# Attention and mixer kernel: the score products of tile i + 2 in front of the value products of tile i

## Chip, cores and metric

The kernel runs on one core of a Trainium2 chip. The metric is the device time of one execution in microseconds (us). Lower is better.

## What is computed

The inputs are q, k and v of 8 batches, 8 heads, 576 positions and 64 channels, and four weight matrices. All are float32, and so is the result.

```python
scores = scale * np.matmul(q, k.transpose(0, 1, 3, 2))
mask = (rel >= 0) & (rel < 64)             # rel = query position - key position
attn = softmax(np.where(mask, scores, -1e9))
x = np.matmul(attn, v)                     # heads side by side: (8, 576, 512)
xt = x.transpose(0, 2, 1)
u = x + (np.maximum(xt @ w_tok1, 0.0) @ w_tok2).transpose(0, 2, 1)
out = u + np.maximum(u @ w_ch1, 0.0) @ w_ch2
```

Each query sees the 64 positions up to its own, so a block of 64 queries needs two blocks of 64 keys.

## The kernel before

**Tiles.** The first stage (the first 256 us) is the attention with the token mixer. It goes over 36 tiles of 128 query rows, numbered 0 to 35. A tile holds two blocks of 64 queries, for all 8 heads. Every ninth tile, with `i % 9 == 4` (4, 13, 22, 31), is shared by two batches: one block of each. The rest of the kernel is the channel mixer, made of large matrix products.

**Steps of one tile**, with the lines that the rows below carry:

- `qk(i)` (L282): the scores, 16 products on quarters of the array (64 rows by 64 columns), into the two PSUM tiles `s`. There are two such buffers of each kind, tag "s".
- `softmax` (L297): VectorE masks the scores and takes the maximum; `softmax_exp` (L305): ScalarE takes the exponentials `e` and their sums.
- `pt_transpose` (L312, L314): TensorE transposes `e` into `pp`, ScalarE copies `pp` to SBUF as `pt`.
- `av(i)` (L324): 16 value products `xp <- v, pt` on halves of the array (128 rows by 64 columns), into the one PSUM buffer `xp`.
- `norm` (L341): VectorE multiplies `xp` with the reciprocals (L335, L336) of the sums, giving `x`.
- `split_x`: ScalarE casts `x` to its high half `xhi` (L109), GpSimd subtracts for the low half `xlo` (L112). In the shared tiles ScalarE makes two casts of 64 rows (L352), one into `xhi` and one into `xlo`, and GpSimd fills the other halves (L353).
- `tok1` (L372): TensorE multiplies `xhi` and `xlo` with the first token weights into the PSUM tiles `h`. When a batch is done, ScalarE and VectorE split `h` (L383, L392).
- a piece of `tok2` (L413, L420): two or three transposes of `x` and six products go into one PSUM buffer `up`; ScalarE copies it out (L425). There is one `up` buffer in this stage, so the first transpose of a piece waits for ScalarE's copy of the piece before it.

Beside this, VectorE, GpSimd and ScalarE convert weights from 64-bit floats and split them (lines L204 to L221, `w1hi`, `w1lo`).

**Order.** Each engine runs its instructions in the order of the program text; nothing reorders them. One round `i` of the loop over tiles issues, on TensorE: transposes of tile i, one piece (A), `tok1` of tile i - 1, value products of tile i, scores of tile i + 2, a second piece (B). On VectorE a round has the softmax of tile i + 1, reciprocals, weight conversion, `norm(i)`, and, where a batch is done, the low half of `h`. On ScalarE it has the two copies to `pt`, a cast of weights, four exponentials of tile i + 1, the copy of piece A, four more exponentials, the cast(s) of `x` of tile i, the copy of piece B. `TOK2_FROM` is 9: the round from which `tok2` pieces run by default.

The two calls that matter stand like this, with the line of `qk` behind that of `av`:

```python
if 0 <= i < NT:
    norm(i, av(i, pts), ri)
finish_h_low()
...
if i + 2 < NT:
    qk(i + 2)
```

Of the kernel before, what the change touches and what calls it, by code (L numbers as in the profile page):

```python
# [27 lines left out]
NT = NPAIR * TPP  # L28
# [17 lines left out]
TOK1_FROM, TOK1_SLOW, TOK2_FROM = 2, 7, 9  # L46
# [34 lines left out]
def tile_blocks(i):  # L81

    p, t = divmod(i, TPP)
    if t == 4:
        return (2 * p, 8), (2 * p + 1, 8)
    b, t = (2 * p, t) if t < 4 else (2 * p + 1, t - 5)
    return (b, t), (b, t + 4)
# [3 lines left out]
def mixer_kernel(ctx: ExitStack, tc: tile.TileContext, qh, kh, vh, wt1, wt2, wc1, wc2, out):  # L91
# [39 lines left out]
    with ExitStack() as actx:  # L131
# [8 lines left out]
        def load_k(i):  # L140
            p, t = divmod(i, TPP)
            if t in (0, 4):
                b = 2 * p + (t == 4)
                kbs[b] = pq.tile([P, NBLK + 1, H // 2, BLK], F32, name=f"k{b}", tag="k", bufs=2)
                if b != 0:
                    nc.sync.dma_start(kbs[b], kh[b])

        def load_q(i):
            qr = pq.tile([P, H // 2, 2, BLK], F32, name=f"q{i}", tag="q", bufs=5)
            nc.sync.dma_start(qr, qh[i])  # L150
            loaded[i] = [qr, None]

        def load_v(i):
            vt = pq.tile([P, 2, H, D], F32, name=f"v{i}", tag="v", bufs=3)
            nc.sync.dma_start(vt, vh[i])
            loaded[i][1] = vt
# [54 lines left out]
        def to_f32_b(c, low, high, n, tag, late):  # L211

            r = cpool[0].tile([P, CW], I32, name=f"r{tag}", tag="cvr", bufs=1)[:, :n]
            w = cpool[0].tile([P, CW], F32, name=f"w{tag}", tag="cvw", bufs=2)[:, :n]
            cf, rf = c.bitcast(F32), r.bitcast(F32)
            nc.vector.scalar_tensor_tensor(out=c, in0=high, scalar=-0x40000000, in1=c,
                                           op0=ALU.bitwise_and, op1=ALU.bitwise_or)
            nc.vector.tensor_scalar(out=r, in0=c, scalar1=-0x800000, scalar2=None, op0=ALU.bitwise_and)
            nc.vector.scalar_tensor_tensor(out=rf, in0=low.bitcast(U32), scalar=2.0 ** -52, in1=rf,  # L219
                                           op0=ALU.mult, op1=ALU.mult)  # L220
            (nc.vector if late else nc.gpsimd).tensor_add(w, rf, cf)  # L221
            return w
# [23 lines left out]
        def job_convert_b():  # L246
            if to_convert_b:
                n, part = to_convert_b.pop(0)
                to_finish.append((n, to_f32_b(*part)))
# [19 lines left out]
        def qk(i):  # L269

            qt = loaded[i][0]
            s = []
            for u in range(2):

                s.append(ps.tile([P, 4, P], F32, name=f"s{i}_{u}", tag="h" if i == 1 else "s", bufs=2))
                s_ps[i, u] = s[u]
            for j in range(4):
                for u in range(2):
                    r = slice(u * BLK, (u + 1) * BLK)
                    for half, (b, n) in enumerate(tile_blocks(i)):  # L280
                        so = s[u][half * BLK:(half + 1) * BLK, j].rearrange("p (n c) -> p n c", n=2)
                        nc.tensor.matmul(so, qt[r, j, half], kbs[b][r, n:n + 2, j],  # L282
                                         start=True, stop=True)

        def softmax(i, u):
            if u == 0:
                st[i] = (pa.tile([P, H], F32, name=f"nm{i}", tag="nm", bufs=3),
                         pa.tile([P, H], F32, name=f"sum{i}", tag="sum", bufs=3))
            nm, sm = st[i]
            mk = mask[1 if tile_blocks(i)[0][1] == 0 else 0]  # L290
            e = pa.tile([P, 4, P], F32, name=f"e{i}_{u}", tag="e", bufs=4)
            e_sb[i, u] = e

            s = s_ps.pop((i, u))
            for h in range(4):
                g = 2 * h + u
                nc.vector.tensor_tensor_reduce(out=e[:, h], in0=s[:, h], in1=mk, scale=-scale, scalar=MAX_F32,  # L297
                                               op0=ALU.add, op1=ALU.min, accum_out=nm[:, g:g + 1])
# [9 lines left out]
        def pt_transpose(i, u):  # L308
            pp = ps.tile([P, 4, P], F32, name=f"pp{i}_{u}", tag="pt")
            e = e_sb.pop((i, u))  # L310
            for h in range(4):
                nc.tensor.transpose(pp[:, h], e[:, h], ident)  # L312
            pt = pa.tile([P, 4, P], F32, name=f"pt{i}_{u}", tag="ptsb", bufs=4)
            nc.scalar.copy(pt, pp)  # L314
            return pt
# [117 lines left out]
        def store_u():  # L433
            while stores:
                us, g0, n = stores.pop(0)
                a = 0
                while a < n:
                    j, o = divmod(g0 + a, CHUNK)
                    m = min(n - a, CHUNK - o)
                    (nc.sync if g0 < (B - 1) * S - 320 else nc.scalar).dma_start(u_dram[j][:, :, o:o + m], us[:, :, a:a + m])  # L440
                    a += m
# [16 lines left out]
        def run_pieces(k):  # L458
            for _ in range(min(k, len(pieces))):
                tok2(*pieces.pop(0))  # L460
# [22 lines left out]
        for i in range(-1, NT + 1):  # L483
            if 0 <= i and i + 2 < NT:
                load_v(i + 2)
            if 3 <= i + 3 < NT:
                load_q(i + 3)
            if i + 4 < NT:
                load_k(i + 4)
            store_u()  # L490
            n_jobs = JOBS[i]
            if i == NT - 1:
                up_tags += [("s", 2), ("pt", 2)]
            have = len(pieces)
            n_pieces = PIECES.get(i, (1, 1) if i >= TOK2_FROM else (0, 0))
            pts = []
            if 0 <= i < NT:
                pts.append(pt_transpose(i, 0))
                if i < NT - 1:
                    pts.append(pt_transpose(i, 1))  # L500
            if i + 1 < NT:
                softmax(i + 1, 0)
            if i + 1 < NT:
                softmax(i + 1, 1)
            if 0 <= i < NT:
                ri = recip(i)
            if i >= N_START:
                while to_finish:
                    job_finish()
            for n in tok1_plan.get(i + 1, ()):  # L510
                last_use = n - NX + ((n - NX) % TPP == 4)
                if n < i and last_use not in tok1_plan.get(i, ()):
                    split_x(n)
            while to_finish:
                job_finish()
            if i + 1 < NT:
                softmax_exp(i + 1, 0)
            run_pieces(min(have, n_pieces[0]))
            have = min(have, len(pieces))
            if i >= N_START:  # L520
                for _ in range(n_jobs):
                    job_convert_a()
            if i == NT - 1:
                pts.append(pt_transpose(i, 1))
            if i < N_START:
                softmax_exp(i + 1, 1)
            for n in tok1_plan.get(i, ()):
                tok1(n)
            if N_START <= i < NT - 1:
                softmax_exp(i + 1, 1)  # L530
            if i >= N_START:
                for _ in range(n_jobs):
                    job_convert_b()
            if 0 <= i < NT:
                norm(i, av(i, pts), ri)
            finish_h_low()
            if i < N_START:
                for _ in range(n_jobs):
                    job_convert_a()
                    job_convert_b()  # L540
            if i + 2 < NT:
                qk(i + 2)
            for n in tok1_plan.get(i + 1, ()):
                if n not in xhl:
                    split_x(n)
            run_pieces(min(have, n_pieces[1]))
            while to_load and len(to_convert) < 2 and i < NT - 2:
                job_load()
            if i == NT - 1:
                while to_convert or to_convert_b or to_finish:  # L550
                    job_convert_a()
                    job_convert_b()
                    job_finish()
                qctx.close()
                pu = uctx.enter_context(tc.tile_pool(name="pu", bufs=1, side="right", reuse_waits="tile"))
                ul = {0: load_u(0, pu)}
# [537 lines left out]
```

## Time and profile before

| | |
|---|---|
| median of 3 runs | 806.01 us (804.53 to 806.02) |
| the profiled execution, its own time | 806.01 us |
| its span, first to last instruction | 804.1 us |
| TensorE products (PE) busy | 789.7 us, 98% of the span |
| TensorE weight loads (PEld) busy | 655.2 us, 81% |
| VectorE (DVE) busy | 567.8 us, 71% |
| ScalarE (ACT) busy | 388.4 us, 48% |
| GpSimd (POOL) busy | 265.1 us, 33% |
| mean granted TensorE clock | 0.999 |

All times are counted from the first instruction. The shares are means over the whole kernel; in the first stage ScalarE and VectorE are much fuller than in the rest. A row of the timeline gives the start, the length, the engine and line, what is written and read, a count of merged instructions, and in brackets how long the engine sat idle before it and what ended that. TensorE's products are pipelined: the spacing of two starts says what a product costs, not its length. A product of float32 operands shows as two records.

### The profile page before, as it was taken

The numbers are of one execution on the slowest core, as the hardware profiler recorded it, in microseconds if no ns is written. First come the engines' busy times: TensorE is split into PE (matmuls) and PEld (weight loads), VectorE is DVE, ScalarE is ACT, GpSimd is POOL, SyncE is SP. The second block draws the span as 40 slices with busy tenths as digits, with TensorE's granted clock in tenths as the row PEclk, the third lists the DMA queues.
The fourth block names the chain that finished last, engine by engine and source line by source line (L and its number), as shares of the span: only waits on it lengthen the run. The fifth ranks groups of instructions, "written<-read, shape, count | busy, mean of one in ns | idle before, by whom it ended". The sixth has DMA issues, their size and how long they took to land. (4 is left out here: it accounts for less than half of the span.)

```text
span 804.1 us, 15810 instructions
## 1 busy us (share of the span) xinstructions
PE 789.7 (98%) x5749; PEld 655.2 (81%) x5749; DVE 567.8 (71%) x1529; ACT 388.4 (48%) x1124; POOL 265.1 (33%) x241
## 2 busy tenths in 40 slices
PE   8999999999999999999999999999999999999997
PEld 6667888888889878888878888888888888888886
DVE  5978789589572895777787474756666666656576
ACT  6998889889874440323334141326332244324040
POOL 3634544445330000000000050549832648723140
PEclk9999999999999999999999999999999999999999
DMA  9856778768635637877555775764985755965543
GB/s 352 274 183 227 231 252 302 236 211 297 218 113 169 198 102 213 255 227 236 196 170 179 281 287 183 246 239 170 315 327 206 287 187 166 364 228 190 199 161 104
DMA packets 86828, 180.59 MB, mean 225 GB/s; under 512 B 8800, under 2 KB 51808, under 8 KB 84832
## 3 DMA queue, kind: packets, MB, share of 16 engines
q1 hardware_dynamic: 84640, 177.76, 64.1%
q10 hardware_dynamic: 2112, 1.84, 0.7%
q8 instruction: 45, 0.74, 0.4%
q14 instruction: 31, 0.25, 0.1%
HBM read 137.69 MB, written 41.88 MB: 223 GB/s over the span
## 5 line engine op out<-in xcount | busy, mean ns | idle before, releaser
L913 PE MATMUL gp<-m,w1hi 128*128 128x512 f32 x504 | 155.8, 390 | 0.4 <-POOL m L794 0.4
L112 POOL TENSOR_TENSOR m7lo<-t3g,m7hi 128x512 fp32r<-128x512 f32 x18 | 23.4, 1302 | 359.5 <-ACT m7hi L109 359.5
L305 ACT ACTIVATE e<-e,nm 128x128 f32<-128x128 f32 x288 | 112.3, 399 | 6.1 <-DVE nm L297 6.1
L913 PEld LDWEIGHTS gp<-m,w1hi 128*128 128x128 f32 x504 | 94.7, 188 | 20.9 <-POOL m L794 1.3
L913 PE MATMUL gp<-m,w1lo 128*128 128x512 f32 x252 | 98.2, 389 | 0.0
L958 DVE TENSOR_TENSOR uf<-op,uf 128x512 f32<-128x512 f32 (+1 forms) x91 | 61.9, 684 | 40.5 <-PE op L969 30.7
L297 DVE CUSTOM_DVE_ANT_0 e<-s,mask 128x128 f32<-128x128 f32 x288 | 63.5, 286 | 12.2 <-PE s L282 12.1
L305 ACT ACTIVATION_READ_ACCUMULATOR e<-e,nm 128x1 f32 x288 | 56.5, 196 | 0.0
L112 POOL TENSOR_TENSOR xlo<-x,xhi 128x512 fp32r<-128x512 f32 x32 | 41.2, 1287 | 46.0 <-ACT xhi L109 45.7
L635 PE MATMUL gp<-uhi,w1hi 128*128 128x512 f32 x144 | 56.1, 389 | 0.0
L635 PE MATMUL gp<-ulo,w1hi 128*128 128x512 f32 x144 | 56.1, 389 | 0.0
L635 PE MATMUL gp<-uhi,w1lo 128*128 128x512 f32 x144 | 56.1, 389 | 0.0
L913 PEld LDWEIGHTS gp<-m,w1lo 128*128 128x128 f32 x252 | 47.3, 188 | 9.7
L643 PE MATMUL op<-ghi,w2hi 128*128 128x512 f32 x128 | 50.0, 390 | 0.9 <-ACT ghi L622 0.9
L643 PE MATMUL op<-glo,w2hi 128*128 128x512 f32 x128 | 50.0, 390 | 0.2 <-DVE glo L623 0.2
L643 PE MATMUL op<-ghi,w2lo 128*128 128x512 f32 x128 | 49.9, 389 | 0.0
L916 ACT COPY x<-gp 128x512 f32<-128x512 f32 x18 | 10.6, 587 | 81.2 <-PE gp L913 81.2
L221 POOL TENSOR_TENSOR w<-r,c 128x384 f32<-128x384 f32 (+1 forms) x28 | 27.6, 985 | 60.5 <-DVE r L219 58.5
L324 PEld LDWEIGHTS xp<-v,pt 128*64 128x64 f32 x1152 | 36.6, 138 | 12.9 <-ACT e L305 10.1
L341 DVE TENSOR_TENSOR x<-xp,ri 128x512 f32<-128x512 f32 x36 | 24.8, 690 | 30.3 <-PE xp L324 29.7
L312 PE MATMUL pp<-ident,e 128*128 128x128 f32 x288 | 44.6, 281 | 1.4
L420 PE MATMUL up<-t2hi,hhi 128*128 128x320 f32 (+1 forms) x128 | 43.0, 336 | 0.0
(204 smaller groups left out, 2042.4 us busy)
## 6 DMA issues: line engine op xcount, KB each, us to landing
v<-vh SPq DMA_DIRECT2D x36, 512.0 KB, 3.8
w1hi<-w1s SPq DMA_DIRECT2D x18, 896.0 KB, 4.9
w1lo<-w1s SPq DMA_DIRECT2D x18, 896.0 KB, 6.9
w1hi<-w2s SPq DMA_DIRECT2D x18, 896.0 KB, 4.6
w1lo<-w2s SPq DMA_DIRECT2D x18, 896.0 KB, 6.4
raw<-wc SPq DMA_DIRECT2D x32, 384.0 KB, 4.4
q<-qh SPq DMA_DIRECT2D x36, 256.0 KB, 4.9
k<-kh SPq DMA_DIRECT2D x7, 1280.0 KB, 8.3
```

The costliest lines, as they stand in the source:

```text
L112: eng_lo.tensor_sub(lo, src, hi.bitcast(F32))
L221: (nc.vector if late else nc.gpsimd).tensor_add(w, rf, cf)
L297: nc.vector.tensor_tensor_reduce(out=e[:, h], in0=s[:, h], in1=mk, scale=-scale, scalar=MAX_F32, op0=ALU.add, op1=ALU.min, accum_out=nm[:, ...
L305: nc.scalar.activation(e[:, h], e[:, h], AF.Exp, bias=nm[:, g:g + 1], scale=-1.0, accum_out=sm[:, g:g + 1])
L312: nc.tensor.transpose(pp[:, h], e[:, h], ident)
L324: nc.tensor.matmul(xp[half * BLK:(half + 1) * BLK, h], pts[h % 2][:, h // 2, half * BLK:(half + 1) * BLK], vt[:, half, h], start=True, sto ...
L341: nc.vector.tensor_mul(x, xp, ri.unsqueeze(2).to_broadcast([P, H, D]))
L420: nc.tensor.matmul(up[:, :n], hx[:, cs], w[:, tt * S + s0:tt * S + s0 + n], start=False, stop=(k == 6), skip_group_check=True)
L635: nc.tensor.matmul(gp, w[:, w1_at(ft, ct)], x[:, ct], start=(k == 0), stop=(k == 3 * NCT - 1))
L643: nc.tensor.matmul(op, w[:, ct, ft], x[:, cols], start=(first and k == 0), stop=(last and k == 3 * len(gs) - 1), skip_group_check=not (fir ...
L913: nc.tensor.matmul(b[INTO[m]], w[:, at], c[:, h, t], start=(k < 4 and z == y == 0), stop=(z == 1 and y == 2), skip_group_check=True)
L958: eng.tensor_add(x, y, x)
```

## The change

From round 9 on, the scores of tile i + 2 are issued before the value products of tile i, and not behind them. In rounds before the ninth nothing changes.

```diff
             if i >= N_START:
                 for _ in range(n_jobs):
                     job_convert_b()
+            if i >= TOK2_FROM and i + 2 < NT:
+                qk(i + 2)
             if 0 <= i < NT:
                 norm(i, av(i, pts), ri)
             finish_h_low()
...
-            if i + 2 < NT:
+            if i < TOK2_FROM and i + 2 < NT:
                 qk(i + 2)
```

On TensorE, in round 22, these rows stand before the change between the last `tok1` product and piece B (a name's first number is the tile, `s24_0` is a score tile of tile 24, `xp22` the value products of tile 22):

```order
L324 MATMUL xp22_2791<-v22_2485,pt22_0_2733 64x64 x8
L324 MATMUL xp22_2791<-v22_2485,pt22_1_2740 64x64 x8
L282 MATMUL s24_0_2810<-k5_2229,q24_2612 64x128 x2
L282 MATMUL s24_1_2811<-k5_2229,q24_2612 64x128 x2
L282 MATMUL s24_0_2810<-k5_2229,q24_2612 64x128 x2
L282 MATMUL s24_1_2811<-k5_2229,q24_2612 64x128 x2
```

And these, on the same engine in the same round, with the change:

```order
L282 MATMUL s24_0_2791<-k5_2229,q24_2612 64x128 x2
L282 MATMUL s24_1_2792<-k5_2229,q24_2612 64x128 x2
L282 MATMUL s24_0_2791<-k5_2229,q24_2612 64x128 x2
L282 MATMUL s24_1_2792<-k5_2229,q24_2612 64x128 x2
L324 MATMUL xp22_2809<-v22_2485,pt22_0_2733 64x64 x8
L324 MATMUL xp22_2809<-v22_2485,pt22_1_2740 64x64 x8
```

The 16 score products have moved in front of the 16 value products (eight rows of scores in all, of which four are shown). The same happens in rounds 9 to 33, 25 in all; rounds 34 and 35 have no scores left to issue.

On ScalarE the same round's rows around the casts of `x` of tile 22 are, before and after alike:

```order
L352 CAST xhi22_2828<-x22_2808 64x512
L352 CAST xlo22_2829<-x22_2808 64x512
L425 COPY u3_0_2720<-up3_0_2_2834 128x256
L314 COPY pt23_0_2857<-pp23_0_2852 128x512
L314 COPY pt23_1_2864<-pp23_1_2859 128x512
```

Nothing moved there: the copy of piece B (`u3_0`) stands behind the casts of `x`, and so it does on VectorE, GpSimd and the DMA queue, whose orders the change leaves as they are.

## Rows read from the trace of the kernel before

**Rows 1.** Stretches: start:end, length, then busy us of PE, PEld, DVE, ACT, POOL.

```profile
156.40:163.00 6.60, 6.47 (x96) 5.54 (x94) 3.74 (x22) 6.58 (x25) 2.53 (x4) 1.00 0.93 329
```

**Rows 2.** Waits of weight loads, 56 to 245 us: us in total, times, longest.

```profile
PEld xp L324 <- ACT e L305: 9.7, 27, 0.4
```

**Rows 3.** Timeline of TensorE, round 25 and the start of round 26.

```profile
173.16 0.39 PE L372 MATMUL h<-xlo,t1hi 128*128 128x512 f32 x1
173.40 0.39 PE L372 MATMUL h<-xhi,t1lo 128*128 128x512 f32 x1
173.71 1.15 PE L324 MATMUL xp<-v,pt 128*64 128x64 f32 x32
174.79 1.10 PE L282 MATMUL s<-k,q 64*64 64x128 f32 x32
175.83 0.44 PE L413 MATMUL up<-ident,x 128*128 128x128 f32 x2
...
177.69 0.38 PE L413 MATMUL up<-ident,x 128*128 128x128 f32 x2
...
178.86 0.39 PE L372 MATMUL h<-xlo,t1hi 128*128 128x512 f32 x1
```

**Rows 4.** Timeline of TensorE, round 34, where no scores follow.

```profile
233.29 1.15 PE L324 MATMUL xp<-v,pt 128*64 128x64 f32 x32
234.38 0.66 PE L312 MATMUL pp<-ident,e 128*128 128x128 f32 x4
```

**Rows 5.** Timeline of VectorE, ScalarE and GpSimd, tile 25.

```profile
175.93 0.29 DVE L297 CUSTOM_DVE_ANT_0 e<-s,mask 128x128 f32<-128x128 f32 x1 [0.33 <-PE s L282]
...
175.64 0.62 ACT L109 CAST xhi<-x 128x512 fp32r<-128x512 f32 x1
177.02 0.37 ACT L425 COPY u<-up 128x256 f32<-128x256 f32 x1 [0.77 <-PE up L420]
...
176.33 1.28 POOL L112 TENSOR_TENSOR xlo<-x,xhi 128x512 fp32r<-128x512 f32 x1 [0.86 <-ACT xhi L109]
```

**Rows 6.** Timeline of ScalarE and TensorE, shared tile 22 and round 23.

```profile
155.08 0.62 ACT L352 CAST xlo<-x 64x512 fp32r<-64x512 f32 x1
...
155.82 0.37 ACT L425 COPY u<-up 128x256 f32<-128x256 f32 x1
...
156.31 1.07 ACT L314 COPY pt<-pp 128x512 f32<-128x512 f32 x2
...
156.50 0.38 PE L413 MATMUL up<-ident,x 128*128 128x128 f32 x2
...
158.45 1.15 PE L324 MATMUL xp<-v,pt 128*64 128x64 f32 x32
```

**Rows 7.** Timeline of ScalarE and weight loads, round 24: cast, copy, next piece.

```profile
162.14 0.62 ACT L109 CAST xhi<-x 128x512 fp32r<-128x512 f32 x1
...
162.65 0.43 ACT L425 COPY u<-up 128x320 f32<-128x320 f32 x1
...
163.13 0.20 PEld L413 LDWEIGHTS up<-ident,x 128*128 128x128 f32 x2 [0.50 <-ACT u L425]
```

**Rows 8.** Timeline of ScalarE and TensorE, shared tile 31.

```profile
215.73 0.62 ACT L352 CAST xlo<-x 64x512 fp32r<-64x512 f32 x1
...
217.42 0.38 PE L413 MATMUL up<-ident,x 128*128 128x128 f32 x2
```

**Rows 9.** Timeline of VectorE, tiles 18 and 19, and of TensorE, piece A behind.

```profile
126.93 0.69 DVE L341 TENSOR_TENSOR x<-xp,ri 128x512 f32<-128x512 f32 x1
...
131.33 1.06 DVE L206 TENSOR_SCALAR c<-c 128x384 f32<-128x384 f32 x1
132.42 0.36 DVE L207 TENSOR_SCALAR c<-c 128x384 int32<-128x384 int32 x1
...
134.35 0.68 DVE L341 TENSOR_TENSOR x<-xp,ri 128x512 f32<-128x512 f32 x1
...
136.48 0.49 PE L413 MATMUL up<-ident,x 128*128 128x128 f32 x3
```

## The prediction

> **What bounds the kernel now.** I read the page first: TensorE's products fill 98% of the span. Then the stretches of the attention stage, where the change lies. In one of 6.6 us TensorE is busy for 6.47 and ScalarE for 6.58 [rows 1]. So two engines are full there, and both run in program order: TensorE sets the time, and ScalarE has almost nothing in hand. What the change can win is only idle time of TensorE. So I asked what its weight loads wait for. The largest entry is the first value product of a tile, put down to ScalarE: 27 waits with 9.7 us together, none longer than 0.4 [rows 2]. That looks like the wait that the move should fill, with scores done while the probabilities are copied. It isn't one. In round 23 the second copy of probabilities ends at 156.31 + 1.07 = 157.38 us and the value products start at 158.45, 1.07 us later [rows 6]. A lead of a microsecond or more stands there in all 25 rounds. The 0.36 us (9.7 / 27) is the same in every round because it is the change of shape: the last full-array product starts at 173.40, the first half-array product at 173.71, a spacing of 0.31 where two full ones stand 0.24 apart (173.16, 173.40) [rows 3].
>
> **What the change removes: nothing that TensorE waits for.** The same 16 score and 16 value products are issued. A round had three changes of shape (full to half, half to quarter, quarter to full) and keeps three (full to quarter, quarter to half, half to full). Of the new ones I find rows for neither end, but the blocks keep their length whatever follows: the value products take 174.79 - 173.71 = 1.08 us ahead of quarter products [rows 3] and 234.38 - 233.29 = 1.09 ahead of full ones [rows 4]. So I take 0 for the swap itself. Bounds: if going from full to quarter needed no more than the plain spacing, a round would win 0.31 - 0.24 = 0.07 us; if it needed twice the extra, it would lose as much. Over 25 rounds that is -1.8 to +1.8 us.
>
> The moved scores now come earlier, so they could wait for their PSUM buffers, which VectorE's masking of the tile before must have left. In round 25 that masking starts at 175.93 and has eight steps of at most 0.29 us, so it ends by 178.25 [rows 5]; even 0.7 later, it ends as `tok1` of round 26 begins (178.86 is its second product [rows 3]), and the scores stand behind all of `tok1`. So this costs 0; it would be seen as a wait of the first score product for VectorE.
>
> **What it adds: x comes later.** The scores' block is 175.83 - 174.79 = 1.04 us long [rows 3], so the value products end 1.04 us later, and VectorE's normalisation starts that much later. Three chains hang on it, and I follow each in a plain round, 25 [rows 3, 5].
>
> 1. VectorE: it no longer waits 0.33 us for the scores, since they are there. The masking starts behind the normalisation, about 0.7 us later than 175.93 (1.04 less the 0.33). The next normalisation is also 1.04 later, so the round's slack covers it. Cost 0.
> 2. GpSimd: the low half of x would start at 176.33 + 1.04 = 177.37 and end at 178.65; the product that reads it starts at 178.86. Cost 0, with 0.2 left.
> 3. ScalarE: the cast of x starts at 175.64 + 1.04 = 176.68. The copy of piece B stands behind it. Two such follow each other by 0.51 us when nothing else holds them (162.14, 162.65 [rows 7]), so the copy starts at 177.19 and not 177.02, and eats 0.17 of the 0.77 us for which ScalarE sat idle. It ends at 177.56. The next piece A, in the one buffer that this copy frees, starts 0.05 us after a copy's end (162.65 + 0.43 = 163.08, then 163.13 [rows 7]), so it could go at 177.61. It goes at 177.69. Cost 0, with 0.08 us left.
>
> So a plain round pays nothing, by a hair. Two kinds of round have less.
>
> *Shared tiles.* Here ScalarE makes two casts, and the copy of piece B followed the second almost at once. In tile 22 the second cast started at 155.08; with 1.04 more it is 156.12, the copy starts 0.51 later at 156.63, ends at 157.00, and piece A can start at 157.05 where it started at 156.50 [rows 6]. TensorE waits 0.55 us. Nothing gives that back: ScalarE is full for the next 6.6 us [rows 1], and TensorE already waits 0.50 for it at their end [rows 7], a wait that moves along with ScalarE. Tile 13 repeats this, 0.55. In tile 31 ScalarE had more in hand: 215.73 + 1.04 + 0.51 + 0.43 + 0.05 = 217.76 against 217.42 [rows 8], so 0.34. Tile 4 lies ahead of the change. Sum: 0.55 + 0.55 + 0.34 = 1.44 us.
>
> *Rounds in which VectorE is the late one.* From the normalisation of tile 18 at 126.93 to that of tile 19 at 134.35 VectorE has no slack, so the second is 1.04 later too: 135.39 + 0.68 (its length) + 0.04 to the cast + 0.51 + 0.43 (the copy) + 0.05 = 137.10, where piece A started at 136.48 [rows 9]: 0.62. But the sum of that stretch may change: one conversion step took 1.06 us where its neighbour of the same size took 0.36 [rows 9], since GpSimd was at work beside it, and VectorE now stands 1.04 later against GpSimd. If the 0.70 goes, the wait goes; if it only falls on another step, all of it stays. I take 0.5, nearer to the upper end since GpSimd works beside VectorE in most of the stage. Tiles 26 to 28 have a late VectorE too; I take 0.3 us for the three together, between 0 and twice that.
>
> The Trainium skill, on the page "Advanced Engine Details and Errata", section VectorE Performance Modes, says that GpSimd instructions and Vector instructions that use both ports block each other. The 1.06 against 0.36 agrees with it. By that rule alone VectorE's lateness is a matter of which steps meet, and the 0.5 and 0.3 could each be 0 or be found in other rounds as well.
>
> Behind the stage nothing changes, and the large products there keep TensorE full, so what the stage loses stays lost. Sum: 0 + 1.44 + 0.5 + 0.3 = 2.2 us. The profiled execution took 806.01 us (span 804.1), which is the median of the three runs too; so 808.2 us. A measurement of this kernel can tell about 0.2% (1.6 us) from no change; 2.2 us is 0.27%.
>
> **The rivals.**
>
> *It is absorbed, no change.* ScalarE might make up its lateness behind a shared tile before the point where TensorE waits for it 0.50 us. Then the 0.55 us of waiting ahead of it only takes the place of that later wait, twice (tiles 13 and 22), and the sum is 2.2 - 1.0 = 1.2: 807.2 us; with VectorE's terms at 0 as well 0.4: 806.4. It decides at the copy of piece B of tile 22: if it is less than 0.5 us late, this rival holds. For it: half a microsecond is little. Against it: ScalarE's 6.58 of 6.60 us. Chance 0.32.
>
> *Faster, by cheaper changes of shape.* If going to quarters costs nothing beyond the spacing, 25 rounds win 1.8 us; with the waits that I count, the end is 806.4, and without them 804.2. Against it: nothing in the rows shows a block whose neighbours change its length. The point is the spacing from the last full product to the first score, under 0.26 against 0.31. That the early scores speed up the softmax speaks for no gain either: VectorE takes them in order, behind the normalisation that is now later. Chance of an end below 804.4: 0.08.
>
> *Slower by more, VectorE late in most rounds.* If the new meetings with GpSimd add 0.3 us or more to VectorE's round, the 0.08 us that plain rounds have in hand are gone, and each of some ten of them pays about 0.2 to 0.3: 2 to 3 us more, 810 to 811. It decides where VectorE's idle time ahead of a normalisation falls to zero in plain rounds. Against it: losing the 0.33 us wait helps VectorE. Chance 0.10.
>
> **How the numbers follow.** The forecast, 807.4 to 809, has a chance of 0.50, the rivals 0.32, 0.08 and 0.10. The time is the forecast's, 808.2. For the range: low end 808.2 - 1.8 (the swap) - 0.8 (VectorE's terms gone) = 805.6; high end 808.2 + 1.8 + 0.3 (tiles 26 to 28 doubled) + 0.5 (a few plain rounds over their 0.08) = 810.8. Slower by over 0.2% means above 807.6: nearly all of the forecast (0.47) and the last rival (0.10), 0.57. Faster 0.08. The rest, 0.35, lies within 0.2%.
>
> **What would show it.** VectorE's wait for scores in front of the masking is gone, and its normalisation stands about 1.04 us later against the last `tok1` product. ScalarE's idle time moves from in front of the copy of piece B to in front of the cast of x. Weight loads of piece A wait for ScalarE's copy in rounds 14, 23 and 32, some 0.5, 0.5 and 0.3 us, and in round 20. The spacing from the last full product to the first score is about 0.31. The stretch behind the stage has its old length. I am wrong if these waits are missing while the time is the same, if the scores wait for their buffers, or if a moved block changes its length.

## The result

The changed kernel took 808.2 us (median of 6 runs, 806.99 to 809.08), the kernel before 805.46 us in as many. The ratio is 1.0033, with a 95% interval of 1.0023 to 1.0044: slower, by 2.7 us. The forecast was 808.2.

The first lines of the page of the changed kernel (busy time, share of the span, instructions):

```profile
span 806.2 us, 15810 instructions
PE 789.9 (98%) x5749; PEld 654.7 (81%) x5749; DVE 569.6 (71%) x1529; ACT 387.4 (48%) x1124; POOL 263.5 (33%) x241
```

The busy times hardly moved, and the span is 2.0 us longer (806.18 against 804.14). The two profiled executions can be cut in three by TensorE's timeline:

| stretch | before | changed |
|---|---|---|
| up to the first transpose of tile 9 | 60.76 | 60.52 |
| from there to the first product of the channel mixer (at 255.82 and 257.96) | 195.07 | 197.45 |
| from there to the end | 548.3 | 548.2 |

So 2.4 us were lost in the stage of the move and none came back behind it. The part ahead of tile 9 is the same code in all kernels of this text, and it took 59.2 to 60.8 us from one profile to another. So the verdicts below go by the measured times, and the readings by round lengths inside the stage, which repeat within 0.05 us where nothing was changed.

The weight loads' waits of the changed kernel, in the stretch of [rows 2], which now ends at 248 us (who waits for whom: us in total, times, longest):

```profile
PEld s L282 <- issue: 3.9, 11, 0.4
PEld up L413 <- ACT u L425: 3.5, 6, 0.8
PEld xp L324 <- ACT e L305: 3.0, 15, 0.4
PEld s L282 <- DVE c L207: 2.1, 6, 0.4
```

The 0.36 us of [rows 2] now stands in front of the first score product and is put down to whoever came by (nobody, or a step of VectorE that had long been done): it belongs to the change of shape and not to an engine. What is new is the second row: the first weight load of a piece waits for ScalarE's copy, 3.5 us in all, where the kernel before had 1.1 us.

A plain round, 25, answers to [rows 3] (TensorE) and [rows 5] (VectorE, ScalarE, GpSimd):

```profile
174.97 0.39 PE L372 MATMUL h<-xhi,t1lo 128*128 128x512 f32 x1
175.29 1.10 PE L282 MATMUL s<-k,q 64*64 64x128 f32 x32
176.32 1.15 PE L324 MATMUL xp<-v,pt 128*64 128x64 f32 x32
177.40 0.44 PE L413 MATMUL up<-ident,x 128*128 128x128 f32 x2
...
179.27 0.38 PE L413 MATMUL up<-ident,x 128*128 128x128 f32 x2
...
180.43 0.40 PE L372 MATMUL h<-xlo,t1hi 128*128 128x512 f32 x1
```

```profile
177.52 0.69 DVE L341 TENSOR_TENSOR x<-xp,ri 128x512 f32<-128x512 f32 x1 [0.60 <-PE xp L324]
178.13 0.28 DVE L297 CUSTOM_DVE_ANT_0 e<-s,mask 128x128 f32<-128x128 f32 x1
...
178.24 0.62 ACT L109 CAST xhi<-x 128x512 fp32r<-128x512 f32 x1 [0.93 <-DVE x L341]
178.77 0.37 ACT L425 COPY u<-up 128x256 f32<-128x256 f32 x1
...
178.94 1.29 POOL L112 TENSOR_TENSOR xlo<-x,xhi 128x512 fp32r<-128x512 f32 x1 [0.93 <-ACT xhi L109]
```

The blocks have traded places and kept their lengths: 0.32 us from the last full product to the scores, 1.03 for the scores, 1.08 for the value products. All 25 rounds show the same within 0.01 us, and so do the 25 of the kernel before, with 0.32 or 0.33 in front of the value products. ScalarE's idle time has moved from the copy of piece B (0.77 in [rows 5]) to the cast of x (0.93). From the last `tok1` product to piece A it is 179.27 - 174.97 = 4.30 us, as before (177.69 - 173.40 = 4.29). The round pays nothing.

The shared tile 22, to be held against [rows 6], and the later wait of [rows 7]:

```profile
156.32 0.62 ACT L352 CAST xhi<-x 64x512 fp32r<-64x512 f32 x1 [1.13 <-DVE x L341]
...
156.96 0.62 ACT L352 CAST xlo<-x 64x512 fp32r<-64x512 f32 x1
...
157.60 0.37 ACT L425 COPY u<-up 128x256 f32<-128x256 f32 x1
...
158.02 0.20 PEld L413 LDWEIGHTS up<-ident,x 128*128 128x128 f32 x2 [0.76 <-ACT u L425]
158.03 0.44 PE L413 MATMUL up<-ident,x 128*128 128x128 f32 x2 [0.52 <-ACT u L425]
```

```profile
164.70 0.20 PEld L413 LDWEIGHTS up<-ident,x 128*128 128x128 f32 x2 [0.50 <-ACT u L425]
```

ScalarE waits 1.13 us for x, makes its two casts, then the copy; TensorE waits for that copy. The weight load in front shows 0.76 us, of which the product shows 0.52 as idle, since the transposes ahead of it still run while their weights are already in. And the wait of round 24 is still there, 0.50 us as in [rows 7]: ScalarE stayed late.

Round lengths, from the first transpose of one tile to that of the next, in us. All rounds from 9 to 34 that are not in the table kept their length within 0.04.

| round | before | changed | difference |
|---|---|---|---|
| 14 (behind shared tile 13) | 5.92 | 6.68 | +0.76 |
| 20 (behind tile 19) | 6.95 | 7.27 | +0.32 |
| 23 (behind shared tile 22) | 6.21 | 6.94 | +0.73 |
| 29 (behind tile 28) | 6.66 | 6.76 | +0.10 |
| 32 (behind shared tile 31) | 5.22 | 5.74 | +0.52 |
| sum | | | +2.43 |

### The profile page after: what moved, and what is told of

Read it like the earlier page. It is cut to its first block, busy times and chain, and to the rows that moved or that the text cites. A ratio compares the mean times of both kernels' runs of the same rounds, so it can differ in the third digit from the quotient of the medians.

```text
span 806.2 us, 15810 instructions
## 1 busy us (share of the span) xinstructions
PE 789.9 (98%) x5749; PEld 654.7 (81%) x5749; DVE 569.6 (71%) x1529; ACT 387.4 (48%) x1124; POOL 263.5 (33%) x241
```

## The experiments

The theory: x is later by one block of scores, ScalarE's copy of piece B stands behind the casts of x, and where ScalarE has nothing in hand (the shared tiles, two casts) TensorE waits for the copy and does not get it back. The rivals: the changes of shape on TensorE got dearer, in all 25 rounds; or VectorE became late in general.

### Which rounds carry the loss: the move undone in three rounds, and made in three alone

`e1_shared_undone`, against the changed kernel:

```diff
-            if i >= TOK2_FROM and i + 2 < NT:
+            if i >= TOK2_FROM and i % TPP != 4 and i + 2 < NT:
                 qk(i + 2)
...
-            if i < TOK2_FROM and i + 2 < NT:
+            if (i < TOK2_FROM or i % TPP == 4) and i + 2 < NT:
                 qk(i + 2)
```

> The changed kernel, with the scores back behind the value products in the rounds of the shared tiles alone (13, 22, 31); the other 22 rounds keep the move. Theory: the loss comes from ScalarE's copy of piece B standing behind two casts of a later x, so it is made in the shared rounds; there it was 0.76 + 0.73 + 0.53 = 2.0 us of the 2.4 us of the stage. This kernel should give those back and keep some 0.4 us (the rounds of tiles 19 and 28): 805.9 against 805.5 for the kernel before and 808.2 for the changed one. Rival, each change of shape on TensorE got dearer: the loss is spread over 25 rounds, 22 of them remain, 22/25 of 2.4 = 2.1 us, so 807.6. Rival, VectorE's lateness in general: most of the loss stays, 807 or more.

Measured: 805.81 us against 805.75 for the kernel before on that chip, ratio 1.0000 (0.9991 to 1.0009). Rounds 14, 23 and 32 are back at 5.99, 6.21 and 5.22 us; rounds 20 and 29 kept 7.25 and 6.74. By round lengths the twenty-two rounds with the move still cost 0.4 us, all of it in rounds 20 and 29, and nothing that the time can tell.

`e2_shared_only` is the other half, the same two conditions the other way round:

```diff
-            if i >= TOK2_FROM and i + 2 < NT:
+            if i >= TOK2_FROM and i % TPP == 4 and i + 2 < NT:
                 qk(i + 2)
...
-            if i < TOK2_FROM and i + 2 < NT:
+            if (i < TOK2_FROM or i % TPP != 4) and i + 2 < NT:
                 qk(i + 2)
```

> The kernel before, with the scores in front of the value products in the rounds of the shared tiles 13, 22 and 31 alone. Theory: three rounds carry nearly the whole loss, about 2.0 us: 807.5 against 805.5, and the waits of piece A's first weight load for ScalarE's copy stand in rounds 14, 23 and 32 as in the changed kernel (0.76, 0.76, 0.54). Rivals (shape changes, or VectorE in all rounds): 3/25 of the loss, 0.3 us, no change that can be measured: 805.8.

Measured: 806.81 us against 805.75, ratio 1.0016 (1.0007 to 1.0025), slower. Rounds 14, 23 and 32 took 6.67, 6.94 and 5.75 us, as in the changed kernel, all others their length of before; the stage grew by 1.9 us. The waits for the copy, in the view of waits:

```profile
PEld up L413 <- ACT u L425: 3.2, 5, 0.8
```

The measured 1.1 us is less than the 2.0 of the theory, which lies at the upper end of the interval; in the profiled execution the three rounds add up to 2.0. Three rounds carry most of the loss, and the rival of 25 rounds falls with both runs.

### Is it the order of copy and casts, or ScalarE's load?

`e3_copy_first`, the changed kernel with the copy of piece B ahead of the casts in the shared rounds:

```diff
+            copy_first = i >= TOK2_FROM and i % TPP == 4
+            if copy_first:
+                run_pieces(min(have, n_pieces[1]))
             for n in tok1_plan.get(i + 1, ()):
                 if n not in xhl:
                     split_x(n)
-            run_pieces(min(have, n_pieces[1]))
+            if not copy_first:
+                run_pieces(min(have, n_pieces[1]))
```

> The changed kernel, with piece B issued ahead of the split of x in the shared rounds, so that ScalarE copies piece B first and makes the two casts behind it. The wait of piece A for that copy in rounds 14, 23 and 32 must go. Theory, ScalarE itself is full there and its lateness moves along: its casts now start only when piece B is done, so it leaves the round about 0.3 us later than in the changed kernel, and TensorE pays in the next place where it waits for ScalarE (round 15: a piece A that already waited 0.64; round 24: 0.50). Total as the changed kernel or up to 0.6 us more: 808 to 808.8. Rival, the only trouble is the order of the copy and the casts (a buffer freed late): the 2.0 us of the shared rounds come back, 806.2.

Measured: 809.41 us, ratio 1.0043 (1.0030 to 1.0056), 1.2 us above the changed kernel and more than the 0.6 that was expected at most. The rows of TensorE and of its weight loads say where it went (rounds 14 and 15):

```profile
95.43 0.38 PE L413 MATMUL up<-ident,x 128*128 128x128 f32 x2
...
97.11 0.50 PE L372 MATMUL h<-xhi,t1hi 128*128 128x512 f32 x1 [0.59 <-POOL xhi L353]
...
101.34 1.28 PE L312 MATMUL pp<-ident,e 128*128 128x128 f32 x8
...
102.29 0.14 PEld L312 LDWEIGHTS pp<-ident,e 128*128 128x128 f32 x1 [0.25 <-ACT e L305]
```

The transposes of round 15 in the changed kernel:

```profile
101.12 1.05 PE L312 MATMUL pp<-ident,e 128*128 128x128 f32 x8
```

Piece A no longer waits in round 14. But the casts come later still, GpSimd's half of `xhi` hangs on them, and `tok1` now waits for that: round 14 takes 6.78 us and not 6.68. ScalarE leaves the round later, and round 15 grows by 0.2 to 8.47: its transposes wait 0.25 us for ScalarE's exponentials, while its piece A waits as long as in the changed kernel (0.64). Round 24 grew by 0.20 at its piece A (0.69 of wait against 0.50), rounds 23, 32 and 33 by 0.12, 0.11 and 0.50: 1.2 us in all six. The expectation had ScalarE's lateness right; it missed GpSimd behind the casts, and in round 15 it named piece A and not the transposes. Turning the order round only picks another victim: x and the copy are both late, and ScalarE has no time for both.

### Taking the load off ScalarE

`e4_cast_on_vector`, the changed kernel with the second cast of the shared tiles on VectorE:

```diff
-                    nc.scalar.copy(t[own], xs[i][own])
+                    if t is xlo and i >= TOK2_FROM:
+                        nc.vector.tensor_copy(t[own], xs[i][own])
+                    else:
+                        nc.scalar.copy(t[own], xs[i][own])
```

> The changed kernel, with the second of the two casts of x in shared tiles 13, 22 and 31 on VectorE instead of ScalarE. VectorE sat idle 3.7 us ahead of the next normalisation in rounds 14, 23 and 32. Theory: ScalarE has 0.64 us less in front of the copy of piece B, so the waits of 0.7, 0.7 and 0.5 us in front of piece A fall to 0 to 0.1, and ScalarE leaves the round no later than in the kernel before: 806.2, 2.0 us less than the changed kernel. Rival (shape changes): 808.2 as before. Rival, VectorE is what counts: it gets more work and the time rises by up to 1 us, 809.

Measured: 805.38 us against 805.75, ratio 0.9997 (0.9988 to 1.0006): the loss is gone, with the move in all 25 rounds. VectorE and ScalarE at tile 13, and TensorE's piece A of round 14, which started at its usual 0.87 us behind the transposes (the edit shifts line numbers by three from there on):

```profile
93.83 0.42 DVE L353 CAST xlo<-x 64x512 fp32r<-64x512 f32 x1
...
93.83 0.62 ACT L355 CAST xhi<-x 64x512 fp32r<-64x512 f32 x1 [0.93 <-DVE x L341]
94.35 0.36 ACT L428 COPY u<-up 128x256 f32<-128x256 f32 x1
...
93.98 1.03 PE L312 MATMUL pp<-ident,e 128*128 128x128 f32 x8
94.85 0.38 PE L416 MATMUL up<-ident,x 128*128 128x128 f32 x2
```

Rounds 14, 23 and 32 fell to 6.20, 6.46 and 5.20 us. The first two stayed 0.28 and 0.25 above the kernel before; in both `tok1` now waits for GpSimd's half of `xhi`, as this weight load in round 14 shows:

```profile
95.92 0.19 PEld L375 LDWEIGHTS h<-xhi,t1hi 128*128 128x128 f32 x1 [0.19 <-POOL xhi L356]
```

Rounds 15 and 24 fell as well, from 8.25 and 8.33 to 7.85 and 7.93, below the kernel before. So part of this gain should be open to the kernel before too.

`e5_before_cast_on_vector` makes the same edit there:

> The kernel before, without the move, with the second of the two casts of x of the shared tiles 13, 22 and 31 on VectorE. It tells how much of the gain of the same edit on the changed kernel belongs to the move. There the rounds 14, 23 and 32 fell by 0.48, 0.48 and 0.54 us, and rounds 15 and 24 by 0.40 each, below their length in the kernel before. Theory: without the move rounds 14, 23 and 32 have nothing to gain (5.9, 6.2, 5.2 us stay), but ScalarE is 0.64 us less late in rounds 15 and 24, where piece A waits 0.64 and 0.50 us for it in the kernel before too: these fall by about 0.4 each. Sum -0.8: 804.9 against 805.75. Rival, those two waits have nothing to do with ScalarE's load in the shared rounds: 805.75.

Measured: 804.89 us against 805.66, ratio 0.9992 (0.9983 to 1.0001). The medians moved by as much as expected, though the interval just includes no change, and the rounds show half of it: 15, 24 and 33 fell by 0.14, 0.14 and 0.15, not two by 0.4. What counts is a pair: rounds 14 and 15 together take 14.21 us before, 14.07 with the cast moved, and 14.05 in the run on the changed kernel. There the first of the pair was still longer and the second shorter, and I had read the second alone. So with the cast on VectorE the move costs nothing at the shared tiles: in the stage the changed kernel is then 0.42 us longer than the kernel before (195.04 against 194.62), which is what rounds 20 and 29 lose (0.32 and 0.10).

### What the rest is: VectorE late in rounds 19 and 28

`e7_jobs_moved` is the changed kernel with the cast on VectorE and two weight conversions moved:

```diff
+JOBS.update({19: 0, 21: 1, 28: 0, 30: 1})
```

> The changed kernel with the cast on VectorE as in the run before it, and with two weight conversions moved: the one of round 19 to round 21, the one of round 28 to round 30 (rounds in which VectorE sat idle 4.0 and 3.4 us). What is left of the loss stands in rounds 20 and 29, 0.30 and 0.10 us. Theory: these come from a normalisation that is late because VectorE has no slack in rounds 19 and 28; without the conversion round 20 falls from 7.25 to 6.95 and round 29 from 6.76 to 6.66, their lengths in the kernel before: 805.0. Rival, they come from something else that the move did in these rounds: both keep their length, 805.4.

The rounds did exactly this: round 20 went from 7.25 to 6.94, round 29 from 6.76 to 6.66, and round 19's normalisation now waits 2.02 us for its products, where VectorE came late before (line numbers are one higher here):

```profile
133.44 0.69 DVE L342 TENSOR_TENSOR x<-xp,ri 128x512 f32<-128x512 f32 x1 [2.02 <-PE xp L325]
```

So these 0.4 us were VectorE's. The stage took 194.7 us, as long as in the kernel before with the cast on VectorE (194.6). The time was 805.70 us, ratio 1.0001 (0.9992 to 1.0009), where 805.0 was expected: the 0.4 us can't be told in the whole, and that this kernel came out 0.8 us above its like without the move has no counterpart in the stage; I leave that open.

### What a change of shape costs

`e6_half_in_front` puts half of the scores (`j` 0 and 1 of 4) ahead of the value products and half behind, one change of shape more in each of 25 rounds. Against the changed kernel, with `qk` taking the range of `j`:

```diff
             if i >= TOK2_FROM and i + 2 < NT:
-                qk(i + 2)
+                qk(i + 2, range(2))
             if 0 <= i < NT:
                 norm(i, av(i, pts), ri)
...
-            if i < TOK2_FROM and i + 2 < NT:
-                qk(i + 2)
+            if i + 2 < NT:
+                qk(i + 2, range(4) if i < TOK2_FROM else range(2, 4))
```

> The changed kernel, with half of the 16 score products in front of the value products and half behind, from round 9 on: one change of shape more in each of 25 rounds (full to quarter to half to quarter to full). It measures the price of a change of shape, which the prediction put at nothing because their number stays at three. In the kernel before, a block of scores lasts 1.04 us, and its eight groups start about 0.09 apart once it runs, 0.72 together: 0.32 for getting in and out. Theory: a plain round grows by about 0.3, the shared rounds' waits shrink to about a third (x is later by 0.5 to 0.6 and not by 1.04): 25 x 0.3 - 1.3 above the changed kernel, about 814. Rival, a change of shape costs no more than the 0.07 us by which the spacing exceeds the plain one: 25 x 0.07 - 1.3 = +0.4, 808.6.

Measured: 809.94 us in two runs, ratio 1.0050 (1.0031 to 1.0068). Neither number was right. TensorE in round 16:

```profile
113.12 0.67 PE L282 MATMUL s<-k,q 64*64 64x128 f32 x16
113.72 1.15 PE L324 MATMUL xp<-v,pt 128*64 128x64 f32 x32
114.80 0.67 PE L282 MATMUL s<-k,q 64*64 64x128 f32 x16
115.40 0.44 PE L413 MATMUL up<-ident,x 128*128 128x128 f32 x2
```

Each half takes 0.60 us where the whole takes 1.04, so the cut costs 0.16 us; plain rounds grew by 0.14 to 0.17 against the kernel before (round 16: 6.93 to 7.09). Rounds 15, 19, 24 and 33 hardly grew, by 0.04 at most. The stage grew by 3.5 us, 0.3 of it in waits for the copy in rounds 14 and 23. The estimate of 0.3 had counted the way in and out of a block fully for each half. So a change of shape is not free, and the prediction's 0 for the swap rests on their number staying three and on the blocks' lengths not hanging on their neighbours, both of which the rounds of the changed kernel show.

### A faster version, without the move

The pairs of rounds behind the shared tiles are set by ScalarE in the kernel before too. `e8_two_casts_on_vector` is that kernel with the edit of e4 and this one:

```diff
-                split(nc.scalar, nc.gpsimd, xhi, xlo, xs[i])
+                split(nc.vector if i in (14, 23, 32) else nc.scalar, nc.gpsimd, xhi, xlo, xs[i])
```

> The kernel before, without the move, with the second cast of the shared tiles 13, 22 and 31 on VectorE and also the single cast of x of the tiles behind them (14, 23, 32), in whose rounds ScalarE has the split of h as well and is full. Theory: TensorE's time in rounds 14 to 15, 23 to 24 and 32 to 33 is ScalarE's; another 0.5 us of its work gone brings up to 0.5 in each of the three pairs. One cast brought 0.14 (14.21 to 14.07 in rounds 14 and 15, 14.54 to 14.40 in 23 and 24), so 0.2 to 0.5 more each: 0.6 to 1.5 us, 803.4 to 804.3 against 804.9 with one cast moved and 805.7 before. Rival: VectorE, which takes on 0.4 to 0.7 us ahead of the split of h and the masking in those rounds, becomes the late one, and the rounds grow: 805.5 or more.

Measured: 804.37 us against 805.51, ratio 0.9987 (0.9978 to 0.9996), just above the 803.4 to 804.3 that was expected. Round 15 fell from 8.15 (with one cast moved) to 7.63, round 24 from 8.19 to 7.84; round 33 stayed at 8.10. Of the two waits of piece A for the copy that the kernel before had, the one in [rows 7] is gone and the one in round 15 fell to 0.08. In that kernel's view of waits they were:

```profile
PEld up L413 <- ACT u L425: 1.1, 2, 0.6
```

`e9_all_casts_on_vector` takes the first cast of the shared tiles away from ScalarE as well (the condition of e4 without `t is xlo`):

> As the run before, and the first cast of the shared tiles 13, 22 and 31 on VectorE too, so ScalarE has no cast of x in the rounds 13, 14, 22, 23, 31 and 32. Theory: if ScalarE still sets the pairs of rounds behind the shared tiles, another 0.1 to 0.3 us in each falls away: 803.0 to 804.2. Rival: by now TensorE's own products or VectorE set them, and nothing is left to win: the time of the run before, within 0.2 us.

Measured: 804.02 us, ratio 0.9979 (0.9970 to 0.9988). But every round has the length that it has in e8, so by the rounds the rival holds: there was nothing left for this cast to win, and the 0.35 us between the two medians is no effect that I can place. Both are faster than both kernels of this text.

## Why the prediction was right

**No wait to remove.** Right. The changed kernel has the 0.36 us in front of whichever block comes first, and rounds without a shared tile or a late VectorE kept their length.

**The swap at 0, with bounds of 1.8 us each way.** Right: the blocks take 1.03 and 1.08 us in the new order as in the old one. The bounds were wider than they had to be.

**Plain rounds at 0, with 0.08 us in hand.** Right, also in its smallness: the copy in round 25 ends at 178.77 + 0.37 = 179.14, and piece A starts at 179.27 as before, 0.87 behind the first transpose. GpSimd's low half ends at 178.94 + 1.29 = 180.23, 0.20 ahead of the product that reads it, as forecast. The scores never waited for their buffers: none of their weight loads waited longer than 0.4 us.

**Shared tiles, 0.55 + 0.55 + 0.34 = 1.44 us.** The mechanism was right and the term too small: 0.76 + 0.73 + 0.52 = 2.01 us. I spaced the copy 0.51 us behind the second cast, as it stands behind a cast of 128 rows in [rows 7]. Here two casts of 64 rows follow each other, and behind each of them the next ScalarE instruction starts 0.64 later (156.32, 156.96, 157.60), not overlapped. That is 0.13 for each; the rest, 0.05 to 0.08, is the start of the piece from a standstill (0.19 us from its transposes to its first product, 158.03 to 158.22, where undisturbed ones have 0.13 or 0.14).

**VectorE's lateness, 0.5 for tile 19 and 0.3 for tiles 26 to 28.** Right in kind, too large: 0.32 and 0.10. Rows of VectorE and GpSimd of the changed kernel, beside [rows 9]:

```profile
128.47 0.69 DVE L341 TENSOR_TENSOR x<-xp,ri 128x512 f32<-128x512 f32 x1
...
131.69 1.02 POOL L112 TENSOR_TENSOR w1lo<-w,w1hi 128x384 fp32r<-128x384 f32 x1 [0.36 <-ACT w1hi L109]
...
131.96 0.77 DVE L335 SCALAR_TENSOR_TENSOR ri<-sum 128x8 f32<-128x8 f32 x1
...
133.24 0.36 DVE L206 TENSOR_SCALAR c<-c 128x384 f32<-128x384 f32 x1
...
135.57 0.68 DVE L341 TENSOR_TENSOR x<-xp,ri 128x512 f32<-128x512 f32 x1
```

And the same two steps in the kernel before:

```profile
130.42 0.41 DVE L335 SCALAR_TENSOR_TENSOR ri<-sum 128x8 f32<-128x8 f32 x1
...
131.16 1.01 POOL L112 TENSOR_TENSOR w1lo<-w,w1hi 128x384 fp32r<-128x384 f32 x1 [0.35 <-ACT w1hi L109]
```

The step that took 1.06 us beside GpSimd took 0.36 now, as the prediction held possible. About half of that came back where GpSimd's subtraction now fell, in the step for the reciprocals (0.41 to 0.77), and the stretch from one normalisation to the next went from 7.42 to 7.10 us. So VectorE made up 0.32 of the 0.62. The prediction leaned to the upper end since GpSimd works beside VectorE in most of the stage; in [rows 1] GpSimd is busy for 2.53 of 6.60 us. The Trainium skill's rule that was named there ("Advanced Engine Details and Errata", section VectorE Performance Modes) agrees as far as this goes: the same instruction was slow where it met a GpSimd instruction and quick where it did not. Whether it uses both ports no row shows. Of tiles 26 to 28 only the last paid.

**The sum.** 2.2 us were forecast, and the stage lost 2.4: one term 0.6 too small, two others 0.4 too large together. That the time met the forecast to the digit is luck: the forecast started from the 806.0 us of three runs, and the median of six is 805.46, so a base 0.5 too high made up for a change 0.5 too small (2.2 us forecast, 2.7 measured, with 1.9 to 3.5 inside the interval).

**The rivals.** Absorbed later: no, the wait of round 24 did not shrink, and taking the load off ScalarE was what brought the time back. Cheaper shapes: no, the spacing from the last full product to the first score is 0.32 and the blocks kept their lengths. VectorE late in most rounds: no, in two.

## What to carry to other kernels

Before moving work forward on a full engine, ask what was made late by it, and follow that through every in-order queue up to the next buffer that the full engine itself needs. Slack in the typical round (here 0.08 us) says little; here the loss sat in five rounds of 25, behind tiles in which an engine had more to do, and what brought it back was to move work off the engine that is late there, not to turn its order round. A wait that shows the same length in every round may be no wait for the engine that is named.

## What the runs showed of the hardware that was not expected

- ScalarE's instructions overlap by some 0.1 us behind a cast of 128 rows (0.51 to 0.53 between starts, 0.62 long). At the shared tiles they did not overlap behind either cast of 64 rows (0.64 between starts, 0.62 long). It isn't the 64 rows alone: with the cast of rows 64 to 127 on VectorE, the copy followed the cast of rows 0 to 63 by 0.52 (93.83 and 94.35 in e4). Why is open.
- VectorE's step that starts while a GpSimd instruction runs can last until that one ends: 131.96 + 0.77 = 132.73 against GpSimd's 131.69 + 1.02 = 132.71 in the changed kernel. The conversion step of [rows 9] ended 0.22 us behind GpSimd's subtraction (132.39 against 132.17).
- One change of array shape more in a round, with the block of scores cut in two, cost 0.16 us in a plain round, half of what the plain pace of the score products had suggested.
- VectorE's cast of 64 x 512 took 0.42 us where ScalarE's took 0.62.
